# A fused attention and MoE kernel: solve steps issued whole and in other slots, two decays moved, the state's update ahead of the outputs, conversions on another engine, and first loads of the last stage issued earlier

## The chip, the cores and the metric

One core of one Trainium2 chip runs the whole program. The metric is the device time of one execution in microseconds (us). The kernel before was timed three times; its profile is of one further execution, with its own time.

## What is computed

The reference runs a recurrent attention over 768 tokens for 4 x 8 heads of 40 elements, then two MLPs over the 3072 tokens with 320 features each:

```python
for t in range(S):
    y[:, :, t] = einsum('bhd,bhde->bhe', r_t, state)
    Sa = einsum('bhde,bhe->bhd', state, a_t)
    state = state * w_t - einsum('bhd,bhe->bhde', Sa, b_t) + einsum('bhd,bhe->bhde', v_t, k_t)
x = (sigmoid(x @ w_gate) * (x @ w_val)) @ w_out          # 320 -> 1536 -> 320
h = x @ w_in                                             # 320 -> 1024
solu = h * softmax(h)
out = ((solu - mean) / sqrt(var + 1e-6) * g_ln) @ w_out   # 1024 -> 320
```

The MLP weights come in as 64-bit floats; the kernel takes each apart as two 32-bit words and makes a 32-bit value of it.

## The kernel before, in words

**Attention in chunks.** The 768 steps are cut into 24 chunks of 32. Two chunks make a superchunk (`SS = 2`), of which there are 12, numbered `n`. Each chunk is worked in two halves of heads (`hs`), so there are 48 pieces `s`, and the program walks through them slot by slot in `slot` (from `s = -6`, ahead of the first piece, to 48). Four slots make one superchunk. For each superchunk a triangular system has to be solved. It is done on VectorE (DVE) in 31 steps `j` by `t_iter`: a product of a column of the result `pT` (PSUM) with a row of the matrix `M` into `tmp` (L258), and the addition of `tmp` to `pT` (L262). For `n` 0 and 2 a step with four or more columns is cut into two halves, which makes four instructions of two. `M` comes from `products`: TensorE (PE) multiplies (`pABK`), ScalarE (ACT) copies to `abn`, the SP queue stores `abn` to DRAM (`ab`), and `t_load` reads it back as `M`. At the end of a solve `t_store` copies `pT` out (`TT`, ACT) and stores it to DRAM (`tt`), and `t_fetch` brings it back as `TB` for the pieces that use it.

**What a slot does.** `slot` has ten places `p`. At each it issues one entry of the list `work` (the matrix work of piece `s`, the outputs `m_y` of piece `s-1`, the state's update `m_state`, the products of piece `s+9`), then a share of the list `back` (VectorE work: solve steps, and the decays of a coming superchunk by `decay`, two scans of some 1.3 us each with a clip and two small ones), and then `fill`, which adds units of the first MLP (`one`, `two` on PE) and pieces of the weights' conversion. The table `SOLVE` says which steps of a solve stand in which of four slots, counted by `k`: for `n` = 1, for `n` = 2, and for all later ones. `WAIT` is a number with no instruction, put at the head of `back` in the slot with `k = 0`:

```python
share, left = [], sum(x for x, _ in back) / (len(work) - p)
while back and (left > 0 or p == len(work) - 1):
    x, f = back.pop(0)
    share.append(f)
    left -= x
```

Every engine and the SP queue run their instructions strictly in the order in which the program writes them (`manual_schedule`).

**Before the first slot** `begin` makes the decays of superchunk 0, then of (1, 0), (1, 1) and (2, 0), each pair being superchunk and half. Solve 0 follows in the slots -6 to -3. In the slots -1 to 5 the first twelve weight blocks are converted (`Convert.value`): four VectorE instructions (L603, L604, L606, L608) and then two on `eng`, which is GpSimd (POOL) (L609, L610).

**Outputs.** `m_y` leaves its result in `yt`; after each fourth piece SP stores it to `xT`. The next block of the MLP reads `xT` as `b_plain`, and `ready` splits it into two parts (`b_tokens`, L539 on ACT and L540 on DVE).

**The rest.** After the slots, `Late.tail` and `Late.first` run the first MLP over what is left of its weights: per unit 16 matmuls into `hid` (L823) and 12 into the accumulators `one`, `two`, `three` (L856 to L858). During block 0 of six, the rest of the first MLP's weights is loaded (`late_...`). From block 1 on, every second unit takes a step of `jobs2`, which converts the second MLP's weights. A step first loads the raw words (`l_cv`, three buffers), and then ACT (L591, L592), DVE and POOL work on them. `Late.second` is the second MLP.

Of the kernel before, what the change touches and what calls it, by code (L numbers as in the profile page):

```python
# [17 lines left out]
ALU = mybir.AluOpType  # L18
# [15 lines left out]
SOLVE = (0, 0, 13, 26, 31), (0, 0, 11, 21, 31), (0, 12, 24, 28, 31)  # L34
WAIT = 2.0
# [21 lines left out]
def run(gen, n=None):  # L57

    if gen is not None:
        for f in itertools.islice(gen, n):  # L60
            f()
# [6 lines left out]
class Attention:  # L68
# [178 lines left out]
    def t_iter(self, n, j):  # L247

        nc = self.nc
        M, TT = self.M[n], self.pT.rearrange("p (j t) -> p j t", t=CH)  # L250
        k, m = CH - 1 - j, j // 2 + 1
        tmp = self.tmp[j % 2][:, 0:m * k].rearrange("p (c t) -> p c t", t=k)

        cut = m // 2 if m >= 4 and n in (0, 2) else 0
        parts = [r for r in (slice(0, cut), slice(cut, m)) if r.stop > r.start]

        def mult(r):
            nc.vector.tensor_tensor(out=tmp[:, r], in0=TT[:, r, j:j + 1].broadcast_to([128, r.stop - r.start, k]),  # L258
                                    in1=M[:, j:j + 1, j + 1:CH].broadcast_to([128, r.stop - r.start, k]), op=ALU.mult)

        def add(r):
            nc.vector.tensor_tensor(out=TT[:, r, j + 1:CH], in0=TT[:, r, j + 1:CH], in1=tmp[:, r], op=ALU.add)  # L262
        return [(0.155 + (r.stop - r.start) * k * 0.00104, lambda r=r, f=f: f(r)) for f in (mult, add) for r in parts]
# [143 lines left out]
    def begin(self, dummy):  # L407
# [26 lines left out]
        for n, hs in ((1, 0), (1, 1), (2, 0)):  # L434
            for f in self.decay(n, hs):
                f()

    def slot(self, s, fill):
# [19 lines left out]
        if pi + 1 < NHS:  # L458
            if pi > 2 * SS:
                self.le_load(pi + 1)  # L460
            m, hs = divmod(pi + 1, 2 * SS)
            if hs < 2 and (m, hs) > (2, 0):
                back += zip((0.5, 1.3, 0.4, 1.3), self.decay(m, hs))
        late = s == -1
        if pi < NHS and not late:
# [9 lines left out]
            lambda: (run(prod), late and self.scaled(pi)),  # L475
            lambda: last and run(self.m_y(s - 1)),
            lambda: on and self.m_state(s),
# [388 lines left out]
class Between:  # L866
# [73 lines left out]
    def fill(self, s, other, flat):  # L940

        p = self.seen[s] = self.seen.get(s, -1) + 1
        if s < FILL:
# [4 lines left out]
            self.cv.eng = self.nc.gpsimd  # L948
# [35 lines left out]
class Late:  # L984
# [80 lines left out]
    def first(self, btw):  # L1065
        nc, acc, hid = self.nc, [x[:, 0:D] for x in (self.lt[:, 0], self.lt[:, 1], self.one, self.three)], self.hid
        nc.sync.dma_start(out=self.gain, in_=self.d["moe2_g_ln"].rearrange("(k p) -> p k", p=128))
        tiles = [range(N0 if b == 0 else NF, 12) for b in range(6)]
# [442 lines left out]
```

## Time and profile before

| what | value |
|---|---|
| median of 3 runs | 1159.73 us (1158.47 to 1161.88) |
| the profiled execution | 1161.03 us, its span 1159.3 us |
| attention with the first part of the first MLP | 0 to about 654 us of the span |
| the rest of the MLPs | about 654 to 1159 us |
| PE, DVE, ACT, POOL busy | 89%, 68%, 51%, 40% of the span |
| mean granted TensorE clock | 0.947 |

The span runs from the first to the last instruction. An engine's busy share is a mean over both parts, which have different limits, so each part has to be read by itself.

### The profile page before, as it was taken

Reading aid. Unit: us, or ns where it says so; the run is one execution under the profiler, and the core shown is the slowest. Engines: PE = TensorE matmul, PEld = TensorE weight load, DVE = VectorE, ACT = ScalarE, POOL = GpSimd, SP = SyncE. Lnnn points to the kernel's source line nnn. Section 1 sums busy time; section 2 is a strip of 40 time slices with the busy share of each in tenths; the row PEclk is TensorE's granted clock in tenths of the full one; section 3 lists DMA queues with packets and bytes.
Section 4 is the critical chain, followed back from the end, with each engine's and each line's share of the span. In section 5 each row is a group of like instructions: output and inputs, shape, how many; then the busy total and the mean of one; then the engine's idle time right before and its main releaser. Section 6 shows DMA issues by size and latency. Waiting matters only on the chain.

```text
span 1159.3 us, 31815 instructions
## 1 busy us (share of the span) xinstructions
PE 1030.9 (89%) x12710; PEld 879.1 (76%) x12710; DVE 792.8 (68%) x2085; ACT 594.5 (51%) x1511; POOL 466.7 (40%) x489
## 2 busy tenths in 40 slices
PE   4287788898999998999999989799999998999997
PEld 2244457777787887888888888688888876888897
DVE  9869899888978879788683235334443369767673
ACT  5245455766666566675666444324343344444542
POOL 7564534446556456464221112234433301322232
PEclk8578998999999999999999989899999999999999
DMA  7564564668666776666534234302211000000001
GB/s 183 140 149 116 140 154 114 143 180 197 169 155 158 192 189 156 156 161 167 129 111 126 68 110 125 105 28 89 85 57 34 1 1 6 19 23 18 18 23 38
DMA packets 179451, 122.62 MB, mean 106 GB/s; under 512 B 106016, under 2 KB 159264, under 8 KB 179296
## 3 DMA queue, kind: packets, MB, share of 16 engines
q1 hardware_dynamic: 179296, 120.52, 40.1%
q8 instruction: 102, 1.67, 0.6%
q14 instruction: 53, 0.43, 0.1%
HBM read 98.94 MB, written 21.53 MB: 104 GB/s over the span
## 4 chain that ended last, share of the span: by engine, by line
PE 50%; DVE 23%; DMA 10%; ACT 7%; issue 4%; SPq 4%; POOL 1%; DVEq 0%; ACTq 0%; POOLq 0%
PE hid L823 20%; DVE pT L262 5%; DVE tmp L258 4%; PE one L823 4%; DMA b_plain<-xT 3%; PE three L1194 2%; DMA M<-ab 2%; PE three L1197 2%; PE three L1195 2%; PE pY L387 2%; DVE RL L374 2%; PE pruv L370 2%; PE two L1181 2%; PE two L856 2%; PE two L858 2%
## 5 line engine op out<-in xcount | busy, mean ns | idle before, releaser
L823 PE MATMUL hid<-l_x,l_w 128*128 128x512 f32 x672 | 161.3, 392 | 0.0
L823 PEld LDWEIGHTS hid<-l_x,l_w 128*128 128x128 f32 x672 | 125.2, 189 | 24.4 <-issue 0.2
L823 PE MATMUL one<-b_tokens,b_w 128*128 128x256 f32 x816 | 128.8, 302 | 2.1 <-DVE b_plain L844 1.7
L258 DVE TENSOR_TENSOR tmp<-pT,M 128x30 f32<-128x30 f32 (+34 forms) x422 | 96.8, 239 | 41.7 <-DMA M<-ab 32.8
L224 POOL TENSOR_TENSOR AT<-abn,mA 64x256 f32<-64x256 f32 x96 | 81.8, 852 | 82.1 <-ACT abn L219 77.2
L823 PEld LDWEIGHTS one<-b_tokens,b_w 128*128 128x128 f32 x816 | 107.7, 197 | 7.8 <-DVE b_plain L844 1.9
L262 DVE TENSOR_TENSOR pT<-pT,tmp 128x30 f32<-128x30 f32 (+34 forms) x422 | 105.2, 249 | 12.3
L540 POOL TENSOR_TENSOR l_x<-l_plain,l_x 128x512 fp32r<-128x512 f32 x43 | 55.6, 1292 | 119.6 <-ACT l_x L539 100.5
L540 POOL TENSOR_TENSOR b_tokens<-b_plain,b_tokens 128x256 fp32r<-128x256 f32 x58 | 47.6, 820 | 125.4 <-ACT b_tokens L539 113.0
L823 PE MATMUL hid<-b_w,l_x 128*128 128x512 f32 x384 | 94.0, 397 | 2.6 <-DVE l_e L1153 2.6
L844 DVE TENSOR_TENSOR l_plain<-hid,l_plain 128x512 f32<-128x512 f32 x43 | 29.7, 691 | 95.1 <-ACT l_plain L843 95.1
L207 PE MATMUL pABK<-AT,BK 128*64 128x64 f32 x768 | 62.4, 239 | 34.9 <-POOL BK L197 33.9
L207 PEld LDWEIGHTS pABK<-AT,BK 128*64 128x64 f32 x768 | 54.5, 150 | 45.7 <-POOL BK L197 36.2
L823 PEld LDWEIGHTS hid<-b_w,l_x 128*128 128x128 f32 x384 | 70.9, 188 | 19.0 <-DVE l_e L1153 3.6
L196 POOL TENSOR_TENSOR AT<-AT,G 40x256 f32<-40x256 f32 x90 | 69.0, 766 | 33.4 <-DVE G L162 19.3
L387 PE MATMUL pY<-RL,YR 128*64 128x32 f32 (+1 forms) x1536 | 59.8, 220 | 24.8 <-DVE RL L374 21.8
L387 PEld LDWEIGHTS pY<-RL,YR 128*40 128x40 f32 (+1 forms) x1536 | 52.1, 131 | 37.3 <-DVE RL L374 22.0
L843 ACT ACTIVATE l_plain<-hid 128x512 f32<-128x512 f32 x43 | 25.6, 595 | 95.2 <-PE hid L823 95.2
L314 ACT ACTIVATE Z<-pu 32x160 f32<-32x160 f32 x192 | 56.2, 293 | 28.6 <-PE pu L311 25.5
L539 ACT ACTIVATE b_tokens<-b_plain 128x256 fp32r<-128x256 f32 (+1 forms) x70 | 33.9, 488 | 63.6 <-DVE b_plain L844 45.5
L370 PE MATMUL pruv<-RL,UV 128*64 128x64 f32 x768 | 58.9, 232 | 6.4 <-ACT YR L237 2.7
L1188 POOL TENSOR_TENSOR l_w<-l_e,l_w 128x1024 fp32r<-128x1024 f32 x12 | 28.8, 2400 | 88.7 <-ACT l_e L1149 51.1
(253 smaller groups left out, 2593.2 us busy)
## 6 DMA issues: line engine op xcount, KB each, us to landing
AT<-in_LA_dram SPq DMA_DIRECT2D x48, 256.0 KB
RL<-in_RS_dram SPq DMA_DIRECT2D x24, 512.0 KB
LB<-in_LB_dram SPq DMA_DIRECT2D x46, 208.0 KB
Z<-in_VN_dram SPq DMA_DIRECT2D x48, 160.0 KB
M<-ab SPq DMA_DIRECT2D x24, 256.0 KB
UV<-in_VT_dram SPq DMA_DIRECT2D x24, 208.0 KB
G<-in_LW_dram SPq DMA_DIRECT2D x22, 214.5 KB
xT<-yt SPq DMA_DIRECT2D x24, 160.0 KB
```

The costliest lines, as they stand in the source:

```text
L196: eng.tensor_tensor(out=at[SROW[g], g], in0=at[SROW[g], g], in1=G[SROW[g]], op=ALU.mult)
L207: yield lambda m=m: nc.tensor.matmul(ps[0:64, m * 64:m * 64 + 64], lhsT=bkt[:, m].rearrange("p s t -> p (s t)"), rhs=at[:, :, m, :], start ...
L224: nc.gpsimd.tensor_tensor(out=at[UROW[g], g].rearrange("p (a b) t -> p a b t", a=2), in0=abn[UROW[g], :, hs], in1=self.mA[UROW[g]].unsquee ...
L258: nc.vector.tensor_tensor(out=tmp[:, r], in0=TT[:, r, j:j + 1].broadcast_to([128, r.stop - r.start, k]), in1=M[:, j:j + 1, j + 1:CH].broad ...
L262: nc.vector.tensor_tensor(out=TT[:, r, j + 1:CH], in0=TT[:, r, j + 1:CH], in1=tmp[:, r], op=ALU.add)
L314: nc.scalar.activation(z[32 * q:32 * q + 32, hs, g, p * 4:p * 4 + 4, :], ps[32 * q:32 * q + 32, 0:160].rearrange("p (h d) -> p h d", d=40) ...
L370: yield lambda p=p, hh=hh, m=m: nc.tensor.matmul(ps[0:64, m * 64:m * 64 + 64], lhsT=uvt[:, hs * 4 + hh, 64 * p:64 * p + 64], rhs=rl[:, hs, ...
L387: yield lambda m=m, g=g, at=at: nc.tensor.matmul(ps[rows[g], m * CH:m * CH + CH], lhsT=flat[:, at:at + rows[g].stop - rows[g].start], rhs= ...
L539: nc.scalar.activation(h, src, AF.Copy)
L540: eng_l.tensor_tensor(out=l, in0=src, in1=h.bitcast(F32), op=ALU.subtract)
L823: nc.tensor.matmul(out, lhsT=a, rhs=b, start=n == 0, stop=n == 7)
L844: self.nc.vector.tensor_tensor(out=self.sg, in0=self.pv, in1=self.sg, op=ALU.mult)
```

## The change

Nothing of the arithmetic changes. The third row of `SOLVE` moves steps 9 to 11 from `k = 0` to `k = 1`, 21 to 23 from `k = 1` to `k = 2`, and 27 from `k = 2` to `k = 3`. `WAIT` is 4.0. All solve steps are issued uncut. The decays of (1, 1) and (2, 0) leave `begin` and join `back` in the slots -6 and -3. `m_state(s)` stands ahead of `m_y(s - 1)`. In slots below 3 the two last conversion instructions go to VectorE. `first` issues three raw loads of `jobs2` at its start.

```diff
-SOLVE = (0, 0, 13, 26, 31), (0, 0, 11, 21, 31), (0, 12, 24, 28, 31)
-WAIT = 2.0
+SOLVE = (0, 0, 13, 26, 31), (0, 0, 11, 21, 31), (0, 9, 21, 27, 31)
+WAIT = 4.0
...
-        cut = m // 2 if m >= 4 and n in (0, 2) else 0
-        parts = [r for r in (slice(0, cut), slice(cut, m)) if r.stop > r.start]
...
+        def mult():
+            nc.vector.tensor_tensor(out=tmp, in0=TT[:, 0:m, j:j + 1].broadcast_to([128, m, k]), in1=M[:, j:j + 1, j + 1:CH].broadcast_to([128, m, k]), op=ALU.mult)
+
+        def add():
+            nc.vector.tensor_tensor(out=TT[:, 0:m, j + 1:CH], in0=TT[:, 0:m, j + 1:CH], in1=tmp, op=ALU.add)
+        return [(0.155 + m * k * 0.00104, f) for f in (mult, add)]
...
-        for n, hs in ((1, 0), (1, 1), (2, 0)):
-            for f in self.decay(n, hs):
-                f()
+        for f in self.decay(1, 0):
+            f()
...
-            if hs < 2 and (m, hs) > (2, 0):
+            if hs < 2 and (m, hs) > (1, 0):
                 back += zip((0.5, 1.3, 0.4, 1.3), self.decay(m, hs))
...
+            lambda: on and self.m_state(s),
             lambda: last and run(self.m_y(s - 1)),
-            lambda: on and self.m_state(s),
...
-            self.cv.eng = self.nc.gpsimd
+            self.cv.eng = self.nc.vector if s < 3 else self.nc.gpsimd
...
         nc.sync.dma_start(out=self.gain, in_=self.d["moe2_g_ln"].rearrange("(k p) -> p k", p=128))
+        for _ in self.jobs2.cv.raw:
+            self.jobs2.load()
```

The order on VectorE at the start, before (G and Q with PE_ copied between them are a decay; `tmp_187<-pT` is the first step of solve 0):

```order
L162 SCALAR_TENSOR_TENSOR G_1_270<-G_1_270,d_150 104x528
L145 TENSOR_SCALAR G_0_292<-G_0_292 104x8x64
L155 SCALAR_TENSOR_TENSOR Q_190<-G_0_292,d_150 104x528
L159 RECIPROCAL d_150<-Q_190 104x8
L160 COPY PE_0_382<-Q_190 104x8
L162 SCALAR_TENSOR_TENSOR G_0_292<-G_0_292,d_150 104x528
L258 TENSOR_TENSOR tmp_187<-pT,M_365 128x31
L262 TENSOR_TENSOR pT<-pT,tmp_187 128x31
```

And of the changed kernel, from step 7 of solve 0 on:

```order
L255 TENSOR_TENSOR tmp_188<-pT,M_365 128x96
L258 TENSOR_TENSOR pT<-pT,tmp_188 128x4x24
L145 TENSOR_SCALAR G_1_270<-G_1_270 104x8x64
L155 SCALAR_TENSOR_TENSOR Q_189<-G_1_270,d_150 104x528
L159 RECIPROCAL d_150<-Q_189 104x8
L160 COPY PE_1_376<-Q_189 104x8
L162 SCALAR_TENSOR_TENSOR G_1_270<-G_1_270,d_150 104x528
L255 TENSOR_TENSOR tmp_187<-pT,M_365 128x115
L258 TENSOR_TENSOR pT<-pT,tmp_187 128x5x23
```

The decay of (1, 1) now stands between steps 7 and 8 of solve 0, and that of (2, 0) behind its last step. Each step is two rows, where steps 6 to 30 were four.

VectorE in a slot with `k = 1` whose outputs are stored to `xT`, before (`yt` is the outputs' result, `Z<-pS` the state's update, `flat` a conversion, `tmp` and `pT` solve steps):

```order
L392 TENSOR_TENSOR yt_4519<-pY_5150,G_1_1742 104x2x4x32
L606 SCALAR_TENSOR_TENSOR flat<-flat 128x224
L258 TENSOR_TENSOR tmp_187<-pT,M_4730 128x121
L262 TENSOR_TENSOR pT<-pT,tmp_187 128x11x11
L333 TENSOR_TENSOR Z_180<-pS_5175,Z_179 40x320 x2
L844 TENSOR_TENSOR b_plain<-one,b_plain 128x256
```

And of the changed kernel:

```order
L329 TENSOR_TENSOR Z_180<-pS_5044,Z_179 40x320 x2
L601 SCALAR_TENSOR_TENSOR flat<-flat 128x224
L255 TENSOR_TENSOR tmp_188<-pT,M_4633 128x126
L258 TENSOR_TENSOR pT<-pT,tmp_188 128x9x14
L388 TENSOR_TENSOR yt_4437<-pY_5068,G_1_1682 104x2x4x32
L839 TENSOR_TENSOR b_plain<-one,b_plain 128x256
```

The outputs have moved behind the state's update and what stood between them. The solve step next to them is step 17 of the solve, where it was step 20.

The SP queue at the start of `first`, before (`in_moe_g_ln_dram` is the first load of `first`; `x2d` and `l_plain<-xT` are results and inputs of the first MLP):

```order
L656 DMA l_plain<-late_moe_w_out 128x320
L1067 DMA b_plain<-in_moe_g_ln_dram 128x8x1
L925 DMA x2d_116<-b_plain 128x2x320
L862 DMA l_plain<-xT_66 128x2x256
L529 DMA l_plain<-xT_66 64x256 x2
```

And of the changed kernel:

```order
L651 DMA l_plain<-late_moe_w_out 128x320
L1062 DMA b_plain<-in_moe_g_ln_dram 128x8x1
L619 DMA l_cv<-in_moe_w_in_dram 128x2x256
L524 DMA l_cv<-in_moe_w_in_dram 64x256 x2
L619 DMA l_cv<-in_moe_w_in_dram 128x2x256
L524 DMA l_cv<-in_moe_w_in_dram 64x256 x2
L619 DMA l_cv<-in_moe_w_in_dram 128x2x256
L524 DMA l_cv<-in_moe_w_in_dram 64x256 x2
L920 DMA x2d_116<-b_plain 128x2x320
```

The three loads stood behind the inputs of block 2 before, at the start of block 1; they now stand a block earlier.

## Rows read from the trace of the kernel before

**Rows 1.** The page's section 1: busy time, share of the span and instructions

```profile
PE 1030.9 (89%) x12710; PEld 879.1 (76%) x12710; DVE 792.8 (68%) x2085; ACT 594.5 (51%) x1511; POOL 466.7 (40%) x489
```

**Rows 2.** The windows view: length, busy PE, PEld, DVE, ACT, POOL; granted clock, DMA

```profile
134.00:186.00 52.00, 39.25 (x646) 27.02 (x642) 48.82 (x165) 24.94 (x74) 21.76 (x25) 0.89 0.46 114
...
422.00:473.00 51.00, 45.13 (x844) 40.16 (x843) 40.07 (x117) 31.63 (x94) 27.85 (x34) 0.93 0.66 162
```

**Rows 3.** The waits of VectorE, 186 to 660 us: total, times, longest

```profile
DVE b_plain L844 <- ACT b_plain L843: 30.1, 19, 3.4
DVE tmp L258 <- DMA M<-ab: 26.3, 8, 4.8
```

**Rows 4.** The chain that ended last, 720 to 768 us: start, length, what

```profile
727.51 3.67 PE hid L823 x16
...
754.58 4.60 PE hid L823 x16
...
760.93 3.65 PE hid L823 x16
...
766.34 1.84 PE hid L823 x8
```

**Rows 5.** The timeline of ACT and PE, 735 to 756 us (in brackets: idle before)

```profile
745.89 0.55 ACT L591 ACTIVATE l_cv<-l_cv 128x384 f32<-128x384 f32 x1 [11.26 <-DMA l_cv<-in_moe_w_in_dram]
...
750.19 0.63 PE L856 MATMUL two<-l_w,l_x 128*128 128x320 f32 x1 [8.21 <-ACT l_x L539]
```

**Rows 6.** The timeline of the SP queue, 680 to 748 us

```profile
683.04 0.42 SPq L1067 DMA_DIRECT2D b_plain<-in_moe_g_ln_dram  x1
690.23 0.36 SPq L925 DMA_DIRECT2D x2d<-b_plain  x1
...
740.95 0.47 SPq L624 DMA_DIRECT2D l_cv<-in_moe_w_in_dram  x1
...
742.63 0.59 SPq L624 DMA_DIRECT2D l_cv<-in_moe_w_in_dram  x1
```

**Rows 7.** The windows view of what reads or writes `tmp`: solves 0, 2, 3

```profile
29.50:54.30 24.80, 21.76 (x112) 0.50 0.57 150
140.20:180.10 39.90, 21.78 (x112) 0.95 0.50 127
186.10:222.40 36.30, 15.85 (x62) 0.92 0.60 149
```

**Rows 8.** The timeline of VectorE, 0 to 75 us

```profile
21.35 0.68 DVE L145 TENSOR_SCALAR G<-G 104x512 f32<-104x512 f32 x1
...
25.36 0.88 DVE L145 TENSOR_SCALAR G<-G 104x512 f32<-104x512 f32 x1
...
29.57 0.19 DVE L258 TENSOR_TENSOR tmp<-pT,M 128x31 f32<-128x31 f32 x1
...
54.19 0.43 DVE L145 TENSOR_SCALAR G<-G 104x512 f32<-104x512 f32 x1
...
70.92 0.19 DVE L258 TENSOR_TENSOR tmp<-pT,M 128x31 f32<-128x31 f32 x1 [6.51 <-DMA M<-ab]
```

**Rows 9.** The timeline of the SP queue, 20 to 72 us: loads of `M`

```profile
24.78 1.16 SPq L529 DMA_DIRECT2D M<-ab  x2
...
65.23 1.14 SPq L529 DMA_DIRECT2D M<-ab  x2
```

**Rows 10.** The longest wait of ACT, 134 to 187 us

```profile
ACT TT L268 <- DVE pT L262: 7.5, 1, 7.5
```

**Rows 11.** The groups of VectorE by line and shape, 80 to 135 us: busy, mean ns

```profile
L606 DVE SCALAR_TENSOR_TENSOR b_plain<-b_raw,b_plain 128x384 f32<-128x384 f32 x5 | 3.2, 643 | 0.1
```

**Rows 12.** The timeline of VectorE and POOL: one shape alone and beside a POOL instruction

```profile
79.34 0.32 DVE L608 TENSOR_SCALAR b_plain<-b_plain 128x320 int32<-128x320 int32 x1
...
105.09 1.19 DVE L608 TENSOR_SCALAR b_plain<-b_plain 128x320 int32<-128x320 int32 x1
...
104.79 1.31 POOL L197 TENSOR_TENSOR BK<-LB,Q 104x512 f32<-104x512 f32 x1
```

More of the change, by code (lines that the diff above doesn't have):

```diff
@@ L252, in t_iter @@
         tmp = self.tmp[j % 2][:, 0:m * k].rearrange("p (c t) -> p c t", t=k)
-        cut = m // 2 if m >= 4 and n in (0, 2) else 0
-        parts = [r for r in (slice(0, cut), slice(cut, m)) if r.stop > r.start]
[L257 to L263, printed above, removed]
+        def mult():
[3 more added lines that the diff above has]
+        return [(0.155 + m * k * 0.00104, f) for f in (mult, add)]
     def t_store(self, n):
```

## The prediction, made before the changed kernel ran

> **What bounds the kernel now.** I read the page's busy shares first: PE 89%, VectorE 68% of the span [rows 1]. That mean hides two stages, so I went to the windows. From 134 to 186 us VectorE is busy 48.82 of 52 us and PE only 39.25; in a later group of four slots (422 to 473 us) it is busy 40.07 of 51 [rows 2]. The waits say what the rest of VectorE's time there is: 26.3 us in 8 waits for the load of `M`, and 30.1 us for ACT [rows 3]. So up to about 600 us the attention runs at VectorE's pace plus the latency of `M`, and VectorE time that disappears from a slot shortens the slot, unless it stood beside one of those waits. After 654 us PE is the bound: `hid` groups follow each other at 766.34 - 760.93 = 5.41 us [rows 4], and only a PE hole can be won. There is one large hole, which the next part opens.
>
> **The late loads: -11.8 us.** At 745.89 ACT takes up the conversion L591 after 11.26 us idle, ended by the landing of `l_cv`; ACT runs in order, so the gate of the next unit waits behind it, and PE stands still for 8.21 us, ended by ACT [rows 5]. What it costs is read from PE's cadence: from the `hid` group at 727.51 to the one at 760.93 there are four units (two of the groups between are not shown, the third is that at 754.58), which takes 33.42 us where 4 x 5.41 = 21.64 are due: 11.8 us. That is more than the hole, because the `hid` group behind it takes 4.60 us and not 3.65 [rows 4]. The change issues the three loads behind the load at 683.04, where the SP queue has nothing until 690.23. One load takes 742.63 - 740.95 = 1.68 us of the queue, three 5.0 us, and 683.46 + 5.0 = 688.5 is before 690.23 [rows 6]: nothing on SP becomes later, and the words are there 50 us before ACT asks for them. What would be late next is the conversion itself: four VectorE instructions and two on POOL stand ahead of the unit's own on these engines, some 4 us (four times 0.64 for the dearest shape of them [rows 11], and two POOL instructions of not over 1.31, the longest that is shown [rows 12]), while PE has 3.7 us of `hid` work and 1.7 us of accumulation (5.41 less 3.67) before it asks. I take the whole 11.8; if the conversion shows, up to half of the 8.2 us comes back, so the bounds are -7.7 and -12.
>
> **Uncut steps: -6 us in solve 2, -7 in solve 0.** A cut solve keeps VectorE busy for 21.76 or 21.78 us in 112 instructions, an uncut one 15.85 in 62 [rows 7]: 5.9 us. Solve 2 stands in 140 to 180 us, where VectorE is the bound [rows 2], and its end is waited for: ACT stands 7.5 us for the last step before it copies `TT` [rows 10]. So I take -6; bounds -3 (half of it refilled by ACT or loads) and -8. Solve 0 runs with nothing between its steps, from 29.57 to 54.19 [rows 8], 24.6 us; its idle pieces are 24.6 - 21.8 = 2.8 us for 112 instructions, 25 ns each, so an uncut one needs 15.85 + 62 x 0.025 = 17.4 us: -7.2.
>
> **The decays: they give back 4 of those 7.** The two stand from 21.35 to 25.36 and from there to 29.57, 4.0 and 4.2 us, just ahead of solve 0 [rows 8]. It seems that 8.2 us go. But solve 0 needs `M`, whose load was issued at 24.78. Of the next one, issued at 65.23, we see the solve begin 5.7 us later, after waiting for it [rows 8, 9]; 24.78 + 5.7 = 30.5, so at 29.57 VectorE had hidden nearly all the latency under the two decays. Moved, they leave VectorE idle until about 29.5, and the decay of (1, 1) comes back between steps 7 and 8: +4.0 us. That of (2, 0) comes behind the last step, where VectorE later idles 6.5 us [rows 8]; it costs nothing while that cover lasts. Solve 0 ends at 29.5 + 17.4 + 4.0 = 50.9 us instead of 54.19: **-3.3**. `TT`, its store, the stores of `ab` and the next `M` stand behind it in one chain, so the first slots move by as much. Bounds: -7 (the decay of (1, 1) hidden) and +1 (POOL's scaling of piece 5 now waits for that decay, 6 us later than before, and could end last).
>
> **The conversions on VectorE: +4 us.** 14 instructions leave POOL: seven blocks of two. Two blocks fall into slot -1, in VectorE's 6.5 us hole (4 x 0.64 = 2.6, with the decay's 4.2 that fills it: no cover is left, but none is owed). The other five fall into slots 0 to 2; eight of their ten instructions lie ahead of the end of solve 1, which the next `M` and all loads behind it on SP wait for. No row shows these on VectorE; the nearest is L606 with two SBUF operands of the same shape, 0.64 us [rows 11]: 8 x 0.64 = 5.1, less about 1 us that VectorE gains where POOL no longer runs beside it: +4. Bounds 0 and +9; the upper one is a rival below. VectorE is held up beside POOL: L608 took 0.32 us once and 1.19 us beside POOL's L197 of 1.31 us [rows 12]. The Trainium skill (SBUF — State Buffer, Who interferes with whom) says that a VectorE instruction with two SBUF inputs and a GpSimd one that reads SBUF exclude each other for a whole instruction, and the later one blocks; by it this part of the change is the wrong way round for the moved instructions, and each would wait for what is left on POOL.
>
> **The other moves: -1 us.** `WAIT` does nothing: the loop pops it at `p = 0` and works out the share anew at `p = 1` from what is left; with 2.0 written back into the changed kernel the order on all engines is the same. Of the solve steps, only step 27 goes to a slot where VectorE waits for ACT (30.1 us in 19 waits [rows 3]); one step is 15.85 / 31 = 0.51 us, in 9 solves -4.6 at most. Steps 9 to 11 and 21 to 23 change places between slots that VectorE bounds: nothing. `m_state` ahead of `m_y` lets PE do the update while it waits for the outputs' operand, but PE is not the bound there; `yt` and its store come some 2 us later behind the update's pieces, less two solve steps that no longer stand ahead of it (1.0 us). I take -2 for the step, +1 for the store: -1, bounds -6 and +5.
>
> **Sum.** -11.8 - 6 - 3.3 + 4 - 1 = -18.1. Against the profiled execution's 1161.03 us (span 1159.3 and 1.7 around it) that is 1142.9; this execution lies 1.3 us above the median of the runs, 1159.73, so the forecast is **1141.6 us**.
>
> **Rivals.** *The waits for `M` shrink too (chance 0.1).* If the moved step and the earlier update let the products of the fourth slot start sooner, half of the 26.3 us [rows 3] may go: 1141.6 - 13 = 1128.6. Against it: solve steps still begin at `p = 1` of the same slot. *The late hole refills (0.1).* The conversion's VectorE and POOL work stands in front of the unit instead of the load: 4.1 of the 8.2 us return, 1145.7. For it: POOL and VectorE run in order; against: later `jobs2` steps leave the 5.41 us cadence as it is. *The moved conversions block on POOL (0.1).* Each of eight waits for a POOL instruction, 0.6 us more on average of up to 1.3 [rows 12]: +5, 1146.6; the slots 0 to 2 would be longer than before. *The outputs' store comes late (0.04).* Place: the slot with `k = 1`; the load of `b_plain`, ACT's split and VectorE's L540 follow the store in order. If all ten blocks lose 2.1 us, and the step of 27 gains nothing, the sum is -11.8 - 6 - 3.3 + 4 + 21 = +3.9, 1163.6, slower. It decides where VectorE waits over 1.5 us for L540 in most blocks; it now waits for other things. *The change does not do what it says:* for `WAIT` that is certain, and priced above.
>
> **Chances.** The forecast's own case has 0.66, from 1134 to 1149 by the bounds of its terms. With the first rival at the low end and the next two inside, I take 1130 to 1150. A measurement can tell about 0.3% from no change, 3.5 us; above 1156.2 lies only the last rival and a rest: faster 0.94, same 0.03, slower 0.03.
>
> **What would show it.** The `hid` cadence at the start of block 1 stays 5.4 us and ACT has no wait for `l_cv`. The last step of solve 0 ends near 51 us, and VectorE is idle from 21 to 29 us. Solve 2 is busy for some 15.9 us and slots 4 to 6 are 6 us shorter. VectorE is busier in slots 0 to 2, and solve 1 ends at about the same time as before. The waits for `M` stay at 2 to 5 us each. The forecast is wrong if the hole in the late part remains, if the groups of four slots from 230 us on change by over 1 us each, or if solve 1 ends over 4 us from where it did.

## The result, and the profile after

The changed kernel took a median of **1143.83 us** (1140.89 to 1146.84, 4 runs), the kernel before, beside it, 1159.96 us: a ratio of 0.986 with a 95% interval of 0.9829 to 0.9891. The forecast was 1141.6 us, range 1130 to 1150. A second set of runs gave 0.9848 (0.9818 to 0.9878). The profiled execution took 1145.02 us, its span is 1143.1 us.

So the total came out as forecast. Its terms did not all do so, and the experiments below tell them apart. First the views of after that answer to the rows of before.

The busy shares of the page of the changed kernel:

```profile
PE 1031.9 (90%) x12710; PEld 879.3 (77%) x12710; DVE 779.3 (68%) x1999; ACT 596.5 (52%) x1511; POOL 456.8 (40%) x475
```

VectorE lost 792.8 - 779.3 = 13.5 us of work [rows 1] and POOL 9.9; PE's work is the same, spread over a shorter span.

The windows of the changed kernel, same columns as [rows 2]:

```profile
134.00:186.00 52.00, 43.17 (x689) 30.81 (x687) 45.22 (x128) 29.10 (x84) 26.46 (x27) 0.87 0.53 126
422.00:473.00 51.00, 47.10 (x905) 42.11 (x904) 40.23 (x117) 33.04 (x97) 28.25 (x35) 0.93 0.67 171
```

Between 134 and 186 us VectorE went from 48.82 to 45.22 us busy while PE got through more (43.17 us against 39.25). In the later window VectorE's share did not move (40.07 and 40.23). Windows at fixed times do not hold the same work in both kernels, since the changed one is ahead by up to 5 us. The slots 4 to 7, in which solve 2 stands, compare like with like; first before, then changed:

```profile
134.12:197.33 63.21, 50.16 (x840) 36.92 (x834) 59.10 (x199) 31.42 (x93) 29.91 (x35) 0.88 0.49 123
```

```profile
135.31:193.14 57.83, 49.13 (x820) 36.52 (x818) 49.64 (x143) 31.57 (x93) 32.71 (x35) 0.88 0.55 134
```

They became 5.4 us shorter. Of the 9.5 us that VectorE works less in them, 5.9 are the uncut solve.

The waits of VectorE from 186 to 660 us, as [rows 3]:

```profile
DVE b_plain L839 <- ACT b_plain L838: 33.8, 18, 3.4
DVE tmp L255 <- DMA M<-ab: 25.7, 8, 5.0
```

The waits for `M` are as they were, 25.7 us for 26.3: nothing of a pause shows from the number 4.0 in place of 2.0.

The windows of what reads or writes `tmp` in solves 0, 2 and 3 of the changed kernel, as [rows 7]:

```profile
31.00:53.00 22.00, 15.96 (x62) 0.50 0.61 152
138.50:175.20 36.70, 15.81 (x62) 0.95 0.51 124
181.80:220.80 39.00, 15.83 (x62) 0.89 0.60 152
```

These solves now cost VectorE 15.8 to 16.0 us in 62 instructions, as was worked out from solve 3 alone.

For the start of the late part: the SP queue of the changed kernel near 680 us, then ACT's conversion of the first words, then PE's `hid` groups in the chain that ended last (as [rows 6], [rows 5] and [rows 4]):

```profile
678.34 0.42 SPq L1062 DMA_DIRECT2D b_plain<-in_moe_g_ln_dram  x1
678.82 0.57 SPq L619 DMA_DIRECT2D l_cv<-in_moe_w_in_dram  x1
...
683.02 1.11 SPq L524 DMA_DIRECT2D l_cv<-in_moe_w_in_dram  x2
685.70 0.37 SPq L920 DMA_DIRECT2D x2d<-b_plain  x1
```

```profile
730.08 0.53 ACT L586 ACTIVATE l_cv<-l_cv 128x384 f32<-128x384 f32 x1
```

```profile
728.46 3.65 PE hid L818 x16
...
733.87 3.65 PE hid L818 x16
...
744.68 3.65 PE hid L818 x16
...
750.09 3.65 PE hid L818 x16
```

The three loads fit between two issues that SP had anyway, 678.82 to 684.13. ACT takes up the words with no wait in brackets, and the groups follow each other at 733.87 - 728.46 = 5.41 us straight through the place where the hole of 8.21 us was.

To place the rest, the table takes from each profiled execution the end of a solve's last step on VectorE, the start of ACT's copy `rn` that begins the work of a slot, and what the span has left after the start of slot 47 (us; the kernels are those of the experiments). Each line is one execution. That of the uncut solves alone took 3.2 us more than the median of its kernel, that of "both back, real pause" 2.4 us less, the others lie within 1.3 us of it; and the two executions of the changed kernel differ by up to 1.9 us in a column.

| kernel | end of solve 0 | slot 0 | end of solve 1 | end of solve 2 | slot 8 | slot 24 | slot 47 | left |
|---|---|---|---|---|---|---|---|---|
| before | 54.28 | 68.34 | 109.89 | 180.02 | 197.33 | 386.18 | 644.41 | 514.9 |
| changed | 52.61 | 68.51 | 110.32 | 175.03 | 193.14 | 385.44 | 639.80 | 503.3 |
| changed, second set | 51.04 | 67.41 | 108.67 | 175.46 | 193.12 | 387.32 | 640.22 | 502.5 |
| late loads only | 56.04 | 69.79 | 110.83 | 182.00 | 199.30 | 387.72 | 645.62 | 503.0 |
| uncut solves only | 49.29 | 63.26 | 105.04 | 172.07 | 187.82 | 378.41 | 639.09 | 516.8 |
| solve 2 uncut only | 54.51 | 68.17 | 108.84 | 175.76 | 192.43 | 383.96 | 644.17 | 513.3 |
| conversions back | 52.14 | 67.54 | 106.90 | 173.94 | 191.88 | 384.13 | 639.47 | 502.4 |
| decays back | 48.56 | 62.28 | 105.22 | 172.56 | 190.54 | 382.25 | 636.37 | 503.3 |
| both back | 49.30 | 63.08 | 102.87 | 168.30 | 186.30 | 378.10 | 636.45 | 503.2 |
| order of outputs back | 51.22 | 66.17 | 109.50 | 176.10 | 193.59 | 383.25 | 637.21 | 502.8 |
| both back, real pause | 48.34 | 61.95 | 101.90 | 168.16 | 185.75 | 377.54 | 628.60 | 503.5 |
| the same, order back too | 49.72 | 63.13 | 104.77 | 170.58 | 187.75 | 375.35 | 625.78 | 503.6 |

Where the 16.2 us of the span went: 514.9 - 503.3 = 11.6 us behind slot 47, and 644.41 - 639.80 = 4.6 us ahead of it. Inside the attention the lead is nothing at slot 0 and at the end of solve 1, 5.0 us at the end of solve 2, 0.7 us at slot 24 and 4.6 us at slot 47.

### The profile page after: what moved, and what is told of

Its sections match the earlier page's. It is cut to its first block, busy times and chain, and to the rows that moved or that the text cites. A ratio compares the mean times of both kernels' runs of the same rounds, so it can differ in the third digit from the quotient of the medians.

```text
span 1143.1 us, 31686 instructions
## 1 busy us (share of the span) xinstructions
PE 1031.9 (90%) x12710; PEld 879.3 (77%) x12710; DVE 779.3 (68%) x1999; ACT 596.5 (52%) x1511; POOL 456.8 (40%) x475
## 4 chain that ended last, share of the span: by engine, by line
PE 60%; DVE 14%; DMA 9%; ACT 8%; SPq 5%; issue 2%; POOL 1%; ACTq 0%; DVEq 0%; POOLq 0%
PE hid L818 21%; PE one L818 6%; PE pruv L366 4%; DVE pT L258 3%; DMA b_plain<-xT 3%; DVE tmp L255 3%; PE pABK L207 3%; ACT YR L237 2%; PE three L1191 2%; PE three L1194 2%; PE three L1192 2%; PE pY L383 2%; PE two L851 2%; PE two L853 2%; PE two L852 2%
## 5 line engine op out<-in xcount | busy, mean ns | idle before, releaser
L255 DVE TENSOR_TENSOR tmp<-pT,M 128x126 f32<-128x126 f32 (+22 forms) x372 | 93.2, 250 | 42.5 <-DMA M<-ab 34.0
L224 POOL TENSOR_TENSOR AT<-abn,mA 64x256 f32<-64x256 f32 x96 | 77.8, 810 | 98.8 <-ACT abn L219 94.2
L258 DVE TENSOR_TENSOR pT<-pT,tmp 128x126 f32<-128x126 f32 (+22 forms) x372 | 96.7, 260 | 10.6
L196 POOL TENSOR_TENSOR AT<-AT,G 40x256 f32<-40x256 f32 x90 | 73.0, 811 | 62.3 <-DVE G L162 47.4
L838 ACT ACTIVATE l_plain<-hid 128x512 f32<-128x512 f32 x43 | 25.7, 597 | 95.4 <-PE hid L818 95.4
L933 PE MATMUL one<-zero 128*128 128x512 bf16 x196 | 64.2, 435 | 2.8 <-DVE lim L96 1.3
L366 PE MATMUL pruv<-RL,UV 128*64 128x64 f32 x768 | 62.0, 239 | 4.1 <-ACT YR L237 2.8
L366 PEld LDWEIGHTS pruv<-RL,UV 128*64 128x64 f32 x768 | 54.3, 150 | 14.0 <-ACT YR L237 4.1
```

The costliest lines, as they stand in the source:

```text
L196: eng.tensor_tensor(out=at[SROW[g], g], in0=at[SROW[g], g], in1=G[SROW[g]], op=ALU.mult)
L224: nc.gpsimd.tensor_tensor(out=at[UROW[g], g].rearrange("p (a b) t -> p a b t", a=2), in0=abn[UROW[g], :, hs], in1=self.mA[UROW[g]].unsquee ...
L255: nc.vector.tensor_tensor(out=tmp, in0=TT[:, 0:m, j:j + 1].broadcast_to([128, m, k]), in1=M[:, j:j + 1, j + 1:CH].broadcast_to([128, m, k] ...
L258: nc.vector.tensor_tensor(out=TT[:, 0:m, j + 1:CH], in0=TT[:, 0:m, j + 1:CH], in1=tmp, op=ALU.add)
L366: yield lambda p=p, hh=hh, m=m: nc.tensor.matmul(ps[0:64, m * 64:m * 64 + 64], lhsT=uvt[:, hs * 4 + hh, 64 * p:64 * p + 64], rhs=rl[:, hs, ...
L933: self.nc.tensor.matmul(self.gv, lhsT=z[:, 0:128], rhs=z, start=True, stop=True)
```

## The experiments

Each kernel was timed beside the kernel before, in three series. The kernels of one series share a chip, so medians are compared only within a series; the median of before was 1162.8 us in the first series, 1162.85 in the second and 1161.72 in the third.

**The late loads alone** (first series). The kernel before with this edit:

```
     def first(self, btw):
         nc.sync.dma_start(out=self.gain, in_=...)
+        for _ in self.jobs2.cv.raw:
+            self.jobs2.load()
```

> The kernel before with one part of the change: the three loads of l_cv are issued at the start of the late part. Theory (PE waited in order behind ACT for these words, so the whole loss in the hid cadence comes back): 11.8 us less than before, ratio 0.990; the 8.2 us hole of PE near 750 us is gone and nothing ahead of 654 us moves. Rival (the hole refills, as the conversion's VectorE and POOL instructions now stand ahead of the unit's own): 7.7 us less, ratio 0.9934, with a PE hole of about 4 us left in the same place. Second rival (the change's whole gain of 16 us is here and the attention's parts cancel): 16 us, ratio 0.986.

Measured: 1150.61 us, ratio 0.990 (0.9876 to 0.9924). The interval leaves out both rivals. Nothing ahead of slot 47 moved forward (645.62 us), and 503.0 us are left behind it, as in the changed kernel. The chain of this kernel in the place of the hole:

```profile
743.40 3.65 PE hid L823 x16
748.81 3.65 PE hid L823 x16
754.22 3.65 PE hid L823 x16
```

The cadence is 5.41 us. This part is worth what was forecast, and all of the kernel's gain behind slot 47 is this part.

The hole itself was 8.2 of these 11.8 us. Most of the rest is the clock of TensorE behind it, which the prediction's rows do not show. PE had run no matmul from 742.0 to 750.2 us. In the windows from 750 to 759 us the granted clock (third number from the end) is then 0.64, between the levels of 1.2 and 2.4 GHz; without the hole it is 1.00. First before, then with the late loads alone:

```profile
750.00:759.00 9.00, 8.36 (x28) 7.05 (x29) 3.49 (x5) 2.17 (x5) 4.75 (x5) 0.64 0.14 44
```

```profile
750.00:759.00 9.00, 9.00 (x48) 7.92 (x47) 3.46 (x8) 3.21 (x7) 2.69 (x3) 1.00 0.10 32
```

From the end of the hole, 750.19 us, to the next `hid` group at 754.37, the twelve matmuls of the accumulation take 4.2 us where they take 1.8 at full clock, with one wait of 0.45 us for POOL among them, and the group behind takes 0.95 us more.

**The uncut solves alone** (first series). The kernel before with `t_iter` as in the diff of the change, where the `cut` is taken out.

> The kernel before with one part of the change: the steps of solves 0 and 2 are not cut. Theory (VectorE bounds the slots 4 to 6, and solve 0 stands alone at the start): solve 0 ends 7.2 us sooner, and solve 2 then 13 us sooner than before; if both are kept to the end, 13 us less, ratio 0.989. Rival (VectorE's gain is lost later because the slots behind wait for another engine or for a load): solve 2 ends about 10 us or more sooner, but the last slot is reached less than 6 us sooner, ratio over 0.995.

Measured: 1154.5 us, ratio 0.9911 (0.9885 to 0.9936), 8.3 us by the medians. The rival's 0.995 is outside, the theory's 0.989 inside. But the sizes are smaller than the theory's: solve 0 began at 31.21 us and ended at 49.29, 18.1 us, where it took 24.7 (6.6 us gained, 7.2 expected), and solve 2 ended 8.0 us sooner, not 13: from the end of solve 1 to the end of solve 2 it is 67.0 us where before it was 70.1, 3.1 us gained for 5.9 us of VectorE work. Slot 47 begins 5.3 us sooner, under the 6 us of the rival; but this execution is the slowest of the kernel's six, 3.2 us above their median, so it does not decide for the rival against the ratio.

With the late loads' 12.2 us this makes about 20 us. The whole change made 16 us, in its second set 18. So **what is left of the change seems to cost 2 to 4 us**. The intervals do not prove such a difference; the next runs look for it.

**Solve 2 alone uncut** (third series), the kernel before with `n in (0,)` for `n in (0, 2)`.

> The kernel before with the steps of solve 2 alone uncut. Theory (VectorE bounds slots 4 to 6): solve 1 ends as before (109.9 us), the stretch from the end of solve 1 to the end of solve 2 is 5.5 to 6 us shorter, and 4 to 6 us are left at the end, ratio 0.995. Rival (given back behind: in the changed kernel the lead was 5.0 us at the end of solve 2 and 0.7 us at slot 24): under 2 us at the end, ratio over 0.998.

Measured: 1159.15 us, ratio 0.9971 (0.9946 to 0.9995). The stretch to the end of solve 2 is 175.76 - 108.84 = 66.9 us, 3.2 us shorter and not 5.5. By whole slots the gain is larger and steadier: slots 4 to 7 take 58.3 us here, 57.6 to 58.9 in all twelve profiles with solve 2 uncut, and 63.2 in both with it cut. The lead is 4.9 us at slot 8 and 0.2 us at slot 47 in this execution. The interval holds both expected ratios, so what is left at the end stays open between 0.6 and 6 us.

**The conversions back on POOL** (first series). The changed kernel with

```
-            self.cv.eng = self.nc.vector if s < 3 else self.nc.gpsimd
+            self.cv.eng = self.nc.gpsimd
```

> The changed kernel with one part undone: the last two instructions of each conversion run on GpSimd again in the slots ahead of 3. Theory (on VectorE they cost what they take while VectorE bounds these slots): solve 1 ends 4 us sooner than in the changed kernel (its 110.3 us), and the whole is 4 us faster than the changed kernel, 1140 us, ratio 0.983. Rival (GpSimd was the later of the two, and the conversions held up its own G and AT products): solve 1 ends later than 110.3 us, and the whole is 2 us or more slower than the changed kernel.

Measured: 1143.37 us, ratio 0.9826 (0.9805 to 0.9848). Solve 1 ended at 106.90 us where the changed kernel's two profiles have 110.32 and 108.67, so at this place the moved instructions cost 1.8 to 3.4 us. Counted from the end of solve 0 it is 54.8 us against 57.7 and 57.6, 2.9 us. At slot 47 it is 0.3 to 0.8 us. The intervals overlap, so a gain of the whole is not shown; that the conversions on VectorE help is not seen anywhere.

**The decays back ahead of solve 0** (first series). The changed kernel with

```
-        for f in self.decay(1, 0):
-            f()
+        for n, hs in ((1, 0), (1, 1), (2, 0)):
+            for f in self.decay(n, hs):
+                f()
...
-            if hs < 2 and (m, hs) > (1, 0):
+            if hs < 2 and (m, hs) > (2, 0):
```

> The changed kernel with one part undone: the decays of (1, 1) and (2, 0) stand ahead of solve 0 again. Theory (VectorE waits 8.3 us for M at the start of solve 0 in the changed kernel, and the decays would stand in that wait): solve 0 starts at the landing of M, about 31 us, and ends at 31.5 + 17.4 = 48.9 us instead of 52.6, and the first slot comes 3 to 4 us sooner; the whole is 3.7 us faster, 1140 us, ratio 0.983. Rival (the first slots wait for something else than TT): solve 0 ends sooner but the first slot starts within 1 us of 68.5 us, and the time stays within 1 us of the changed kernel.

Measured: 1141.83 us, ratio 0.9821 (0.9798 to 0.9845). Solve 0 ended at 48.56 us (48.9 expected), slot 0 came at 62.28 us, 5.1 to 6.2 us sooner than in the two profiles of the changed kernel, and slot 47 3.4 to 3.9 us sooner. The rival is out by the place of slot 0; the ratio's interval still overlaps those of the changed kernel. The timelines of VectorE show why the moved decays cost more than they take. First the changed kernel, then the one with the decays back (its lines lie one further down there, L606 for L605):

```profile
31.46 0.19 DVE L255 TENSOR_TENSOR tmp<-pT,M 128x31 f32<-128x31 f32 x1 [8.30 <-DMA M<-ab]
...
52.43 0.18 DVE L258 TENSOR_TENSOR pT<-pT,tmp 128x16 f32<-128x16 f32 x1
52.52 0.42 DVE L145 TENSOR_SCALAR G<-G 104x512 f32<-104x512 f32 x1
...
55.68 0.40 DVE L145 TENSOR_SCALAR G<-G 104x512 f32<-104x512 f32 x1
...
63.02 0.56 DVE L604 TENSOR_TENSOR b_plain<-b_plain 128x384 f32<-128x384 f32 x1
63.61 0.56 DVE L605 TENSOR_TENSOR b_raw<-b_plain 128x384 f32<-128x384 f32 x1
...
67.43 0.86 DVE L604 TENSOR_TENSOR b_plain<-b_plain 128x384 f32<-128x384 f32 x1
68.32 1.43 DVE L605 TENSOR_TENSOR b_raw<-b_plain 128x384 f32<-128x384 f32 x1
69.67 0.18 DVE L255 TENSOR_TENSOR tmp<-pT,M 128x31 f32<-128x31 f32 x1
```

```profile
30.51 0.16 DVE L255 TENSOR_TENSOR tmp<-pT,M 128x31 f32<-128x31 f32 x1
...
48.47 0.42 DVE L145 TENSOR_SCALAR G<-G 104x512 f32<-104x512 f32 x1
...
59.32 0.56 DVE L606 TENSOR_TENSOR b_raw<-b_plain 128x384 f32<-128x384 f32 x1
64.13 0.19 DVE L255 TENSOR_TENSOR tmp<-pT,M 128x31 f32<-128x31 f32 x1 [4.26 <-DMA M<-ab]
```

In the changed kernel VectorE idles 8.30 us for `M` ahead of solve 0, where the two decays used to stand; that of (1, 1) comes back inside solve 0. Behind the last step there are two decays where there was one, then twelve conversion instructions, and the first step of solve 1 comes with no wait: VectorE is now the later one, where `M` used to be (6.51 us of wait [rows 8]; 4.26 us are back in the second fence). But slot 0 waits for something else. POOL, PE and ACT of the changed kernel from 50 to 69 us:

```profile
55.84 2.37 POOL L196 TENSOR_TENSOR AT<-AT,G 40x256 f32<-40x256 f32 x2 [4.16 <-DVE G L162]
58.30 2.40 POOL L197 TENSOR_TENSOR BK<-LB,Q 104x512 f32<-104x512 f32 x1
...
67.95 1.38 POOL L197 TENSOR_TENSOR BK<-LB,Q 104x512 f32<-104x512 f32 x1
```

```profile
60.75 1.11 PE L207 MATMUL pABK<-AT,BK 128*64 128x64 f32 x8 [8.63 <-POOL BK L197]
...
67.49 0.49 PE L293 MATMUL pr<-Z,AT 128*32 128x40 f32 x32
```

```profile
66.74 1.23 ACT L237 ACTIVATE YR<-pBK 64x160 f32<-64x160 f32 x4 [1.47 <-PE pBK L232]
...
68.51 0.30 ACT L296 ACTIVATE rn<-pr 128x160 f32<-128x160 f32 x1
```

POOL waits 4.16 us for the decay of (2, 0) and scales that piece until 60.70. Its two groups take 2.37 and 2.40 us there, where the same shapes took 1.42 and 1.18 us at 47.43 and 48.92 us; VectorE's next decay and the conversions run beside them, but what lengthens them was not tested. PE stands 8.63 us for this piece, and PE does its work in order: `pBK` and the products `pr` of slot 0 come behind it, and ACT, in order too, waits for `pBK` before it comes to `rn`. The second profile of the changed kernel has the same waits of 4.16 and 8.63 us. With the decays back PE takes up that piece at 51.74 us and `pr` runs at 58.19. Slot 0 then waits for something else: ACT was held by an earlier store of `ab` and comes to `rn` only at 62.28 us:

```profile
59.19 0.78 ACT L219 ACTIVATE abn<-pABK 64x256 f32<-64x256 f32 x2 [5.51 <-DMA ab<-abn]
```

So slot 0 begins 68.51 - 52.61 = 15.9 us after the end of solve 0 in the changed kernel and 62.28 - 48.56 = 13.7 us with the decays back: 2.2 us through POOL, PE and ACT. Solve 0 itself takes 21.2 us against 18.1, 3.1 us for the decay of (1, 1) inside it. The remaining 0.9 us is the start of solve 0, 31.46 and 30.51 us; in the table's executions it lies anywhere from 29.6 to 31.7, with the decays at either place.

**The changed kernel once more** (second series), for comparison.

> The changed kernel itself, as the measure for the runs beside it on this chip. Theory and rival alike: ratio to before between 0.983 and 0.989, as in its first runs.

Measured: 1144.5 us (1143.68 to 1147.18), ratio 0.9848 (0.9818 to 0.9878).

**Both back** (second series): the two edits above together.

> The changed kernel with two parts undone, the conversions on VectorE and the moved decays. Theory (each of the two costs the first slots time, in the same chain from solve 0 to solve 1, and nothing behind gives it back): solve 0 ends near 48.6 us, solve 1 near 102 us, the gains add up, 5 to 7 us faster than the changed kernel, ratio about 0.980. Rival (they are not additive, since the first slots then wait for PE's or ACT's work): at or above the better of the two alone, within 1 us of the kernel with only the decays put back.

Measured: 1141.25 us (1140.05 to 1141.58), ratio 0.981 (0.9786 to 0.9834). That is 3.3 us below the changed kernel beside it, and the runs of the two do not overlap. Solve 1 ended at 102.87 us, 5.8 us sooner than beside it and 2.4 us sooner than with the decays alone, yet slot 47 begins where it does with the decays alone (636.45 and 636.37). So in these executions the theory holds to the end of solve 1 and the rival at the end: the conversions' part is gone by slot 47, the decays' part stays. That the two moves together cost time is shown by the runs that do not overlap; the ratios 0.981 and 0.9821 do not tell the kernel with both back from that with the decays back.

**The outputs ahead of the state's update again** (second series). The changed kernel with two lines of `work` exchanged:

```
-            lambda: on and self.m_state(s),
             lambda: last and run(self.m_y(s - 1)),
+            lambda: on and self.m_state(s),
```

> The changed kernel with one part undone: the outputs' products stand ahead of the state's update again. Theory (the order of the two pays nothing where VectorE bounds, and the outputs' store comes about 1 us sooner): within 2 us of the changed kernel. Rival (the state's update is the chain from slot to slot and earlier is better): 3 us or more slower than the changed kernel, above all in slots 36 to 47 where PE bounds.

Measured: 1142.93 us (1141.77 to 1144.28), ratio 0.9834 (0.981 to 0.9858), 1.6 us below the changed kernel beside it, in runs that just overlap; slot 47 begins 3.0 us sooner. The rival is out: the exchange of the change pays nothing. What it does is in the waits of ACT, first of the changed kernel beside it, then with the order of before:

```profile
ACT b_tokens L534 <- DMA b_plain<-xT: 26.2, 8, 6.3
```

```profile
ACT b_tokens L534 <- DMA b_plain<-xT: 17.2, 7, 3.9
```

With the later store of the outputs ACT waits 9 us more for the words that it splits, and ACT is in order. Most of it is in two blocks, 6.3 and 5.9 us near 216 and 264 us against 3.9 and 3.7; with the pause of the next run they are 5.5 and 6.0 us, and 3.2 and 3.7 with this exchange added. Slots 8 to 11, where the first of them falls, take 48.1 and 48.8 us in the two profiles of the changed kernel and 46.4 here. Other waits of ACT move the other way (for `UV` 23.9 and 31.7 us), so that the store causes the 1.6 us is likely and not shown.

**A pause that works** (second series). With both parts back, the solve steps of the first slot (`k = 0`) of solves 4 to 11 are kept from the first four of its ten places:

```
-            while back and (left > 0 or p == len(work) - 1):
+            while back and (left > 0 or p == len(work) - 1) and not (n > 3 and k == 0 and p < 4):
```

> The kernel with both parts undone, and in addition a pause that does what the number only says: in the first slot of solves 4 to 11 no solve step is issued ahead of the fifth of the slot's ten places. Theory (VectorE, in order, stands at the first step for M while its other work for the slot is queued behind): the 8 waits for M, 26 us in the changed kernel, fall below 5 us, and 8 to 20 us go, ratio 0.963 to 0.973. Rival (the waits stood beside ACT's and PE's chain anyway): the waits for M go and others on ACT or PE take their place, less than 3 us gained. Second rival (slower): the steps pushed back end later, so TT and all behind it come later by up to 1 us a solve, 8 us lost.

Measured: 1136.2 us (1133.85 to 1137.35), ratio 0.9773 (0.9749 to 0.9797): 5.0 us below the kernel without it beside it, in runs that do not overlap. Up to the end of solve 3 the two kernels are the same, and the table has them within 1.2 us to slot 24; the gain comes behind it, 7.9 us at slot 47 in these two executions, which are the slowest of the one kernel and the fastest of the other. The waits of VectorE from 186 to 660 us, without the pause and with it:

```profile
DVE b_plain L840 <- ACT b_plain L839: 33.8, 19, 3.4
DVE tmp L255 <- DMA M<-ab: 22.4, 7, 5.5
DVE RL L370 <- PE pruv L366: 17.2, 12, 3.0
```

```profile
DVE b_plain L840 <- ACT b_plain L839: 38.2, 25, 3.4
DVE RL L370 <- PE pruv L366: 23.1, 18, 3.0
...
DVE tmp L255 <- DMA M<-ab: 2.7, 3, 1.7
```

19.7 us of waits for `M` went, 4.4 + 5.9 = 10.3 us of them came back as waits for ACT and PE. The result lies between theory and rival: half of the wait stood in front of work that was not ready anyway, and a quarter of it, 5 us, became time.

**The pause, and the outputs first** (third series): the last two edits together.

> The changed kernel with three parts undone (conversions on VectorE, moved decays, the state's update ahead of the outputs) and the pause that works. Theory (the later outputs' store delays the split of b_plain on ACT and VectorE in the blocks where ACT waits for that load, by 1 to 2 us in some blocks): 2 us faster than the kernel with the pause alone, ratio 0.975. Rival (where the pause fills VectorE's wait, the order of outputs and update pays nothing any more): within 1 us of it, ratio 0.977.

Measured: **1131.36 us** (1126.09 to 1132.68), ratio 0.9733 (0.9701 to 0.9766). This beats both kernels: the changed kernel's two ratios are 0.986 and 0.9848. Against the kernel with the pause alone (0.9773) the intervals overlap; the profile has slot 47 at 625.78 us, 2.8 us sooner, although its solve 0 ended 1.4 us later.

**The row of steps as before** (third series), in the kernel just named:

```
-SOLVE = ..., (0, 9, 21, 27, 31)
+SOLVE = ..., (0, 12, 24, 28, 31)
```

> The kernel beside it (three parts undone, working pause) with one more part undone: the solve steps in the slots of solves 3 to 11 are split as before, 12, 12, 4, 3. Theory (the split only moves step 27 out of the first two slots' sums and three steps from the first slot to the third; VectorE pays a step the same everywhere): within 1.5 us of the kernel beside it. Rival (the row is part of the gain, since VectorE waits for ACT in the slot that takes step 27): 3 us or more slower than it. Second rival: faster by 2 us or more, since the first slot takes more steps and the later slots wait less.

Measured: 1136.54 us (1135.24 to 1140.79), ratio 0.979 (0.9759 to 0.9821): 5.2 us slower than the kernel beside it, runs apart. So the first rival's time came. Its reason is not shown, nor is that twelve steps are too many for the six places left of the first slot: the edit moves steps in all four slots at once. What the row is worth without a pause was not tried.

**A longer pause** (third series), `p < 6` for `p < 4`.

> The kernel with three parts undone and a pause of six places of ten in place of four. Theory (M lands by the third place, so four places already hide it and two more only press nine steps, 4.2 us, into the last four places): no gain, 0 to 3 us slower than with four. Rival (VectorE's work of the slot is still held up by steps in the fifth and sixth place): 2 us or more faster.

Measured: 1142.3 us (1138.69 to 1145.17), ratio 0.9839 (0.9808 to 0.987): 10.9 us slower than with four places, where at most 3 were expected. The waits of VectorE from 186 to 660 us have no `M` any more, and the one for PE's outputs is longer; with four places, then with six:

```profile
DVE yt L388 <- PE pY L383: 13.5, 9, 2.8
```

```profile
DVE yt L388 <- PE pY L383: 23.7, 13, 2.8
```

Solve 6 now ends at 359.69 us instead of 356.25. That the steps which are pressed into the last places stand in front of other work of VectorE fits this; no run separates it from the rest.

## Why the prediction was right, and where it was not

*What bounds the kernel*: right for slots 4 to 7, which VectorE's lighter work made shorter, and for the late part. "VectorE's pace plus the latency of `M`" up to 600 us was too simple: when 19.7 us of the waits for `M` went, 5.0 us of time went, since ACT and PE were nearly as late.

*The late loads, -11.8*: right. 11.6 us by the spans behind slot 47, 12.2 us by the medians of the kernel with this part alone. Neither refilling of the hole nor a late conversion shows. The reason given for 11.8 being more than the hole's 8.2, one `hid` group of 4.60 us, covers 0.95 of the 3.6 us; most of the rest is the accumulation ahead of that group, at the granted clock of 0.64.

*Solve 2, -6*: the size was off, inside its bounds. Its stretch is 5.4 us shorter in the first profile of the changed kernel and 3.3 us in the second (66.8 us), 3.1 and 3.2 us in the two kernels that only take out cuts. By whole slots, 4 to 7, it is 5.4 and 4.7 us in the changed kernel, 5.1 and 4.9 in those two, so nearly what was forecast. ACT's wait for the last step, which was 7.5 us [rows 10], is 3.1 us.

*Solve 0 with the decays, -3.3*: here a step failed. To the end of solve 0 the sum was right (50.9 us forecast; 52.61 and 51.04 measured, the first because the load of `M` was issued at 26.51 us and not at 24.78). But "it costs nothing while that cover lasts", said of the decay of (2, 0), did not hold. The step looked at VectorE alone, whose idle time there did take the decay (52.52 to 55.68 us). It left out who waits for the decay: POOL's scaling of that piece, PE's product behind it, and in PE's order `pBK` and the first products of slot 0, for which ACT waits. POOL's wait was reckoned for the decay of (1, 1) alone, as a bound. This is 2.2 us, and slot 0 began at 68.51 and 67.41 us where 3 us sooner than 68.34 were forecast. On VectorE the cover was as short as forecast: the four moved instructions of slot -1 took 0.56 + 0.56 + 0.86 + 1.43 = 3.4 us for 2.6, and the first step of solve 1 came at 69.67 us with no wait ahead of it. Putting the decays back shows the price: 5 to 6 us at slot 0, of which 2.2 are this step and 3.1 the decay of (1, 1) that was priced at 4.0; 3.4 to 3.9 us at slot 47.

*The conversions, +4*: right in place, smaller in size, 2.9 us from the end of solve 0 to the end of solve 1; eight instructions of 4.6 us stand ahead of it, 5.1 forecast. Two of the eight were held up beside POOL, for 0.4 us together, where the rival had 5 (its row, [rows 12], is of an instruction with one input, the moved ones have two). Of the kernel's time the move costs less, and nothing that is clear.

*The other moves, -1*: the sign was wrong for the exchange of outputs and state. It costs 1.6 us by medians that are near the limit of what can be told. The rival of the outputs' late store, which had 0.04, names what ACT's waits for that load show; the cost is 1.6 us where the rival had up to 21. Early on the exchange seems to help: with the conversions on POOL, slot 0 to the end of solve 1 takes 39.4 to 40.0 us in the three kernels with the state's update first and 40.6 to 41.8 us in the seven with the outputs first. That `WAIT` does nothing was right; the working pause shows that a real one is worth 5 us in the kernel with both parts back.

*What slots 8 to 47 do with a lead*: the forecast carried each microsecond from the first slots to the end. In the profiled executions the leads of 9.5 us (uncut solves alone) and 11.0 (both back) at slot 8 shrink to 5.3 and 8.0 at slot 47. That the kernels lose this is not shown. By the medians the uncut solves are worth 8.3 us, and both back, less the late loads, 21.6 - 12.2 = 9.4 us, within 2 us of the leads. The granted clock from slot 8 to slot 36 was 0.97 before and 0.95 in these two executions, and a group of four slots at a lower clock is mostly the longer one (slots 20 to 23, the same code: 46.97 us at 0.96 before, 50.66 at 0.93 with the late loads alone). Whether the clock falls because the work is spread otherwise, or by chance, is open. The forecast's own test, groups of four slots equal within 1 us, was too fine: the kernel with the late loads alone has the same code there, and between slots 16 and 24 it differs from before by 3.0 us one way and, in the next group, 3.7 us the other.

*Total*: attention -4.6 us (-6.3 forecast) and late part -11.6 us (-11.8). With the right sizes the terms would be about -11.6 for the loads and -8 for the solves, and some 3 to 5 us back for the decays, the conversions and the exchange. That the attention's sum came so near is partly luck. Slot 0 came at most 0.9 us sooner where 3.3 were forecast, and from slot 0 to the end of solve 1 nothing was lost (41.8 and 41.3 us, 41.6 before) where 4 were; at the end of solve 1 the two misses cancel.

## What to carry to other kernels

Work that stands under a load's latency (the decays under that of `M`) is free there; moved behind it, it is not. An idle stretch of an engine covers a moved step only if nobody waits for that step's result: follow it through the other engines' orders, here from VectorE over POOL and PE to ACT. And check what a constant does in the code before believing its name: the pause that paused nothing was worth 5 us once it did, at four places, and six places were 11 us slower than four. An idle stretch of PE can also cost more than its length, by the lower clock behind it: here 11.8 us for 8.2.

## What the runs showed of the hardware

The same VectorE instruction L605 on two operands in SBUF took 0.56 us alone and 1.43 us when it began at 68.32 us, while POOL's L197 ran from 67.95 to 69.33. It ended at 69.75, 0.42 us after POOL. Four of the 14 moved instructions were longer than alone, and each of them ended 0.35 to 0.42 us after the POOL instruction beside which it began. The Trainium skill (SBUF — State Buffer, Who interferes with whom) says that such a pair excludes each other and the later one is blocked for the whole instruction; by it they would end 0.48 to 0.56 us after POOL, and the trace agrees to about 0.14 us. The four lost 1.6 of the 9.1 us that the 14 took, so little of the time hung on it: moving the work to VectorE cost mainly what VectorE needs for it.

TensorE's granted clock was 1.00 from 727.5 to 742 us in the kernel before and 0.64 from 750 to 759 us, after 8.2 us without a matmul; the same `hid` group took 4.60 us there and 3.65 otherwise.

A load of `M` from its issue to the first step that reads it took 31.46 - 26.51 = 4.95 us ahead of solve 0, with VectorE waiting for it. In the kernel with both parts back VectorE waited for such loads seven times from 186 to 660 us, up to 5.5 us; with a pause of four places three times, up to 1.7 us.
